# Fifteen loads of 1 to 15 rows of 64 bytes, put into the load queue between the first two K pieces and the first V piece

## The chip, the cores and the metric

The kernel runs on one core of a Trainium2 chip. The metric is the device time of one launch in microseconds (us). Engines are called as the profile calls them: PE (matrix multiply), DVE (vector), ACT (scalar activation), POOL, and SP, which here does nothing but issue loads. Loads move over the core's 16 DMA engines.

## What is computed

One decoding step, two batch rows (B = 2), everything in float32. Cut to what matters:

```python
xn = layernorm(x)                                   # x: 2 x 1 x 512
q = (xn @ wq)                                       # 32 heads of 128
p = softmax(einsum(q, k_cache) * 128**-0.5)         # k_cache: 2 x 32 x 8192 x 128
s = einsum(p, v_cache) @ wo                         # v_cache: the same shape
h = gelu(layernorm(xn) @ w1 + b1)                   # 512 -> 1376
g = silu(h @ w2 + b2)                               # 1376 -> 512
out = x + s * g
```

The two caches are 268 MB each, read once: nearly all of the 559 MB that the kernel reads.

## The kernel before

The caches are cut into N = 32 pieces each, of two heads: a piece is 128 partitions x 64 KB, 8.4 MB. K pieces go in turn to `big0` and `big1` (`KBUF`), V pieces to `big2` (`VB`). For every piece DVE multiplies K in place by q and reduces (`scores`, L319), PE and DVE find the maximum, ACT takes the exponentials, PE multiplies them with V (`weighted`, L466) and transposes the result. After the last V piece `wo` is loaded into `big2` in eight parts, and the projection ends the kernel.

Nearly all loads are issued by SP, in the order in which the program writes them, and a load that has to wait holds back all behind it:

- at the start the tail of `w2`, `w1`, `wq`, K piece 0 and the rest of `w2` (L202 to L212), one right behind the other;
- K piece 1 (L298), which waits for PE's last q product, because `wq` lies in its buffer;
- two loads of x into the tile `x4` (L299 to L301), each of 4 rows of 512 bytes;
- a wait (L304) for PE's last setup product (`pgate`), because the setup's operands lie in `big2`, and then V piece 0 (L305);
- from there in turn K piece n + 2, when PE is past the maximum of piece n (`p_k`), and V piece n + 1, when PE has read V piece n (`p_free`);
- at the end the last V piece in halves, `wo`, and the store of the output, with a wait for it (L373 to L375).

A load raises its semaphore by 16 when it is complete. `op` (L47) issues one instruction, `wait` (L39) only waits; both go through a helper, so the views show L51, L50 and L41 for nearly everything, and groups are told apart by their tiles.

Of the kernel before, what the change touches and what calls it, by code (L numbers as in the profile page):

```python
# [13 lines left out]
class Program:  # L14
# [24 lines left out]
    def wait(self, eng, *tokens):  # L39
        for name, v in self.need(eng, tokens):  # L40
            self.engines[eng].wait_ge(self.sem(name), v)  # L41
# [5 lines left out]
    def op(self, eng, method, *args, waits=(), sig=None, by=1, quiet=False, **kwargs):  # L47
        need = self.need(eng, waits)
        for name, v in need[:-1]:
            self.engines[eng].wait_ge(self.sem(name), v)  # L50
        ins = getattr(self.engines[eng], method)(*args, **kwargs)  # L51
        for name, v in need[-1:]:
            ins._wait_ge(self.sem(name), v)
        if quiet:
            return None
        name = sig or "own_" + eng
        by = 16 if method == "dma_start" else by
        ins.then_inc(self.sem(name), by)
        self.counts[name] += by
        return name, self.counts[name]  # L60


def decode_kernel(nc, x, kc, vc, wq, wo, w1, b1, w2, b2, out):
# [32 lines left out]
    op, wait, take = pr.op, pr.wait, pr.take  # L96

    def sb(shape, name):
        return nc.alloc_sbuf_tensor(name, list(shape), F32).ap()

    def ps(shape, name):
        return nc.alloc_psum_tensor(name, list(shape), F32).ap()
# [63 lines left out]
    rl = sb([P, B], "rl")  # L166
    on = sb([P, MB, OC], "on")
    mod_b = sb([P, R], "mod_b")

    bank = [ps([P, 512], f"bank{i}") for i in range(8)]  # L170
    po = bank[0]
# [18 lines left out]
    def pe(name):  # L190
        return "pe_setup", PE_EVENTS.index(name) + 1

    def pe_n(name, n):
        return name, n + 1

    t = {}
# [30 lines left out]
    for k in (7, 6, 1, 2, 4, 0):  # L227
# [13 lines left out]
                  op=ALU.add)  # L241
# [59 lines left out]
                     waits=[t["x4m"]])  # L301


    wait("SP", t["sel"], t["qnat"], pe(PE_EVENTS[-1]))  # L304
    op("SP", "dma_start", VB, vf[0], sig="d_v")  # L305
    for n in range(N - 2):
# [35 lines left out]
    with nc.scalar.Fori(0, N // U) as i:  # L342
        for u in range(U):
# [4 lines left out]
            for s in range(U):  # L348
# [19 lines left out]
                 op=ALU.mult, waits=[t["rl"], t["on0"], pe_n("p_oa", 0)])  # L368
# [3 lines left out]
    t["res"] = op("DVE", "tensor_add", res, res, x4, waits=[a, t["x4"]])  # L372
    t["out"] = op("SP", "dma_start", out.rearrange("b s (j n) -> j (b s) n", n=P), res[::HB, :], sig="d_out",  # L373
                  waits=[t["res"]])
    wait("SP", t["out"])  # L375


    done = []
# [23 lines left out]
    for c in range(ND):  # L402
# [4 lines left out]
        j, k = NF % QT, NF // QT  # L407
# [6 lines left out]
    j, k = NF % QT, NF // QT  # L414
    mm(ph[R * j:R * j + B, k * P:k * P + FT], ones[:1, :B], b1_sb[:, NF * P:], start=False, stop=True, sig="ph")
    by_tile = ident.rearrange("p (j r) -> p j r", r=R)
    for k in range(NH):
        n = min(QT, NF + 1 - k * QT)
# [16 lines left out]
    for g in range(N // NPB):  # L435
        mm(PB[g % len(PB)], sides, QN[:, g * NPB:(g + 1) * NPB, :].rearrange("h n d -> h (n d)"),
           waits=[t["side"], t["QN rest" if g else "QN first"]] + ([t[f"Q{QH}"]] if g >= len(PB) else []),
           sig=f"pb{g}")
    for f in range(NF + 1):
        j = f % QT  # L440
        k = P if f < NF else FT
# [3 lines left out]
    for j in range(QT):  # L445
        mm(pgate[R * j:R * j + MB, :], mod_b[:, :MB], g_nat[:, j * P:(j + 1) * P], waits=[t["g"], t["mod_b"]],
           sig="pgate" if j == QT - 1 else None)
# [64 lines left out]
    for b in range(B):  # L512
        h = slice(b * H, (b + 1) * H)
        mm(OA[:, b, :OC], Z[:, h].rearrange("p h r -> p (h r)"), mod, waits=[t["Z"]],
           sig="p_oa" if b == B - 1 else None)
# [45 lines left out]
```

## Time and profile before

| | us |
|---|---|
| median of 3 runs | 1300.24 |
| the three runs | 1300.05, 1300.24, 1301.04 |
| profiled execution, span from first to last instruction | 1298.7 |
| median less span (what lies around it) | 1.5 |
| PE busy | 461.9 (36%) |
| DVE busy | 1135.7 (87%) |
| ACT busy | 72.0 (6%) |
| DMA queue of SP and its packets, share of 16 engines | 99.7% |
| bytes read | 559.30 MB, 431 GB/s over the span |

The page's slices cut a span into 40 equal parts; a digit 9 says that the engine was busy for 90% of the slice or more. The same 40 slices are printed for any shorter window, so a window of 60 ns has slices of 1.5 ns and shows single packets. A packet is counted in the window in which it starts, with its whole duration and all its bytes; in a short window the share can so go over 100%, and GB/s far over what the engines move. The profiled execution's own time is not listed apart from the three runs.

### The profile page before, as it was taken

The numbers are of one execution on the slowest core, as the hardware profiler recorded it, in microseconds if no ns is written. First come the engines' busy times: TensorE is split into PE (matmuls) and PEld (weight loads), VectorE is DVE, ScalarE is ACT, GpSimd is POOL, SyncE is SP. The second block draws the span as 40 slices with busy tenths as digits, with TensorE's granted clock in tenths as the row PEclk, the third lists the DMA queues.
The fourth block names the chain that finished last, engine by engine and source line by source line (L and its number), as shares of the span: only waits on it lengthen the run. The fifth ranks groups of instructions, "written<-read, shape, count | busy, mean of one in ns | idle before, by whom it ended". The sixth has DMA issues, their size and how long they took to land. (4 is left out here: it accounts for less than half of the span.)

```text
span 1298.7 us, 7184 instructions
## 1 busy us (share of the span) xinstructions
PE 461.9 (36%) x2958; PEld 148.9 (11%) x2958; DVE 1135.7 (87%) x171; ACT 72.0 (6%) x245; POOL 2.1 (0%) x14
## 2 busy tenths in 40 slices
PE   3813434322433322343322344322334321333337
PEld 1201111001111000111000111100111100111103
DVE  2599999988889988889988888988888988888991
ACT  1100000000000000000000000000000000000000
POOL 0000000000000000000000000000000000000000
PEclk8756776667777567777556767656776666677659
DMA  9999999999999999999999999999999999999998
GB/s 412 436 426 444 424 440 430 426 446 424 444 426 430 440 426 446 424 442 426 426 446 426 444 426 438 430 426 446 426 444 424 438 432 426 446 424 442 416 432 360
DMA packets 11242, 559.38 MB, mean 431 GB/s; under 512 B 1264, under 2 KB 1536, under 8 KB 1892
## 3 DMA queue, kind: packets, MB, share of 16 engines
q1 hardware_dynamic: 11228, 559.30, 99.7%
q8 instruction: 3, 0.05, 0.0%
q14 instruction: 3, 0.02, 0.0%
q10 hardware_dynamic: 8, 0.01, 0.0%
HBM read 559.30 MB, written 0.00 MB: 431 GB/s over the span
## 5 line engine op out<-in xcount | busy, mean ns | idle before, releaser
L51 DVE TENSOR_TENSOR big<-big,Q 128x16384 f32<-128x16384 f32 (+1 forms) x33 | 551.3, 16707 | 73.5 <-DVEq L45 73.5
L51 DVE TENSOR_REDUCE sc<-big 128x128 f32<-128x16384 f32 (+1 forms) x33 | 551.2, 16703 | 4.8
L51 PE MATMUL bank<-big,PZ 128*8 128x512 f32 x2048 | 292.5, 735 | 629.2 <-PEq L45 629.2
L51 PEld LDWEIGHTS bank<-big,PZ 128*8 128x8 f32 x2048 | 60.5, 103 | 833.8 <-issue 833.8
L51 PE MATMUL bank<-Q,ident 128*128 128x512 f32 (+2 forms) x198 | 78.6, 507 | 0.2 <-issue 0.2
L51 ACT COPY o<-bank 128x512 f32<-128x512 f32 x33 | 19.3, 585 | 893.3 <-ACTq L45 881.7
L51 PE MATMUL bank<-ident,MX 128*1 128x128 f32 x32 | 9.2, 286 | 136.7 <-PEq L45 136.7
L51 PE MATMUL bank<-mod,o 128*128 128x2 f32 x256 | 32.8, 250 | 27.4 <-PEq L45 27.4
L51 PEld LDWEIGHTS bank<-mod,o 128*128 128x128 f32 x256 | 31.0, 191 | 55.4 <-issue 55.4
L51 PEld LDWEIGHTS bank<-Q,ident 128*128 128x128 f32 x198 | 33.6, 197 | 16.5 <-issue 16.5
L51 ACT ACTIVATE PZ<-sc,bias 64x128 f32<-64x128 f32 x64 | 25.5, 399 | 6.6 <-ACTq L45 6.2
L51 DVE TENSOR_REDUCE nm<-bank 1x2 f32<-1x128 f32 x32 | 8.9, 279 | 18.8 <-DVEq L45 18.8
L51 DVE TENSOR_TENSOR big<-big,mine 64x512 f32<-64x512 f32 (+1 forms) x2 | 4.5, 2279 | 21.8 <-ACT big L51 21.8
L51 PEld LDWEIGHTS bank<-ident,MX 128*1 128x1 f32 x32 | 2.5, 79 | 161.7 <-issue 161.7
L51 ACT COPY bias<-bank 128x1 f32<-128x1 f32 x32 | 5.1, 159 | 223.6 <-ACTq L45 223.6
L51 PE MATMUL bank<-big,sides 64*128 64x512 f32 x16 | 12.6, 962 | 3.7 <-DVE big L51 3.7
L51 PE MATMUL bank<-nm,srow 1*64 1x1 f32 x128 | 10.2, 216 | 9.8 <-PEq L45 9.4
L51 DVE TENSOR_REDUCE MX<-sc 128x1 f32<-128x128 f32 x32 | 9.2, 286 | 4.7
L51 PE MATMUL bank<-big,xnT 128*2 128x512 f32 x64 | 9.2, 744 | 10.6 <-DMA big<-in_A_wq_dram 10.6
L51 ACT ACTIVATION_READ_ACCUMULATOR PZ<-sc,bias x64 | 11.8, 185 | 0.0
L51 DVE SCALAR_TENSOR_TENSOR res<-bank,gate 128x128 f32<-128x128 f32 x1 | 0.3, 292 | 12.1 <-PE bank L51 12.1
L51 PEld LDWEIGHTS bank<-nm,srow 1*64 1x64 f32 x128 | 8.5, 160 | 16.1 <-issue 16.1
(78 smaller groups left out, 74.7 us busy)
## 6 DMA issues: line engine op xcount, KB each, us to landing
big<-in_A_k_cache_dram SPq DMA_DIRECT2D x2, 4096.0 KB, 35.9
big<-in_A_v_cache_dram SPq DMA_DIRECT2D x2, 4096.0 KB, 36.0
big<-in_B_w_dram SPq DMA_DIRECT2D x1, 2752.0 KB, 10.3
big<-in_B_w_dram SPq DMA_DIRECT2D x1, 2560.0 KB, 52.4
big<-in_A_wo_dram SPq DMA_DIRECT2D x1, 2560.0 KB, 14.9
big<-in_A_wo_dram SPq DMA_DIRECT2D x1, 2048.0 KB, 19.4
big<-in_A_wo_dram SPq DMA_DIRECT2D x1, 1536.0 KB, 22.6
big<-in_A_wo_dram SPq DMA_DIRECT2D x1, 1024.0 KB, 24.3
```

The source lines that it names most:

```text
L51: ins = getattr(self.engines[eng], method)(*args, **kwargs)
```

## The change

Between the two loads of `x4` and the wait before V piece 0, SP issues fifteen more loads. Load k (k from 1 to 15) brings 16 k values of x as k rows of 16 values, 64 bytes, into column block k of partitions 0 to k - 1 of a new tile `spare` (16 partitions x 1 KB). That makes 120 rows and 7,680 bytes. Nothing reads `spare`. The last wait of SP also asks that the fifteen loads are complete (15 x 16 = 240).

```diff
+    spare = sb([16, 16, 16], "spare")
...
+    for k in range(1, 16):
+        op("SP", "dma_start", spare[:k, k, :], x[0, 0, :16 * k].rearrange("(k n) -> k n", k=k), sig="d_spare")
     wait("SP", t["sel"], t["qnat"], pe(PE_EVENTS[-1]))
     op("SP", "dma_start", VB, vf[0], sig="d_v")
...
-    wait("SP", t["out"])
+    wait("SP", t["out"], ("d_spare", 240))
```

## Rows read from the trace of the kernel before

**Rows 1.** The page: busy us of the engines, DMA in 40 slices, SP's load queue.

```profile
PE 461.9 (36%) x2958; PEld 148.9 (11%) x2958; DVE 1135.7 (87%) x171; ACT 72.0 (6%) x245; POOL 2.1 (0%) x14
...
DMA  9999999999999999999999999999999999999998
...
q1 hardware_dynamic: 11228, 559.30, 99.7%
```

**Rows 2.** The DMA in 100 to 1200 us: totals, and issue to landing (median us).

```profile
DMA packets 8191, 476.98 MB, mean 434 GB/s; under 512 B 912, under 2 KB 912, under 8 KB 912
big<-in_A_v_cache_dram SPq DMA_DIRECT2D x29, 28.0
big<-in_A_k_cache_dram SPq DMA_DIRECT2D x28, 40.9
```

**Rows 3.** Timeline of SP, 0 to 110 us: start us, us, what it issued.

```profile
0.73 0.88 SPq L51 DMA_DIRECT2D big<-in_B_w_dram  x2
1.65 2.14 SPq L51 DMA_DIRECT2D big<-in_A_wq_dram  x1
...
40.70 0.33 SPq L51 DMA_DIRECT2D big<-in_A_k_cache_dram  x1
41.07 1.23 SPq L51 DMA_DIRECT2D x<-in_A_x_dram  x2
66.43 0.33 SPq L51 DMA_DIRECT2D big<-in_A_v_cache_dram  x1
```

**Rows 4.** The instructions that write or read tile x: duration ns min/median/max, starts.

```profile
L51 SPq DMA_DIRECT2D x<-in_A_x_dram x2: 509/588/668, 41.1 to 41.8; - x2
```

**Rows 5.** The DMA in 73.40 to 74.10 us (slices of 17.5 ns).

```profile
DMA  0000109109000990010199000091010990090000
DMA packets 40, 0.79 MB, mean 1129 GB/s; under 512 B 20, under 2 KB 28, under 8 KB 28
```

**Rows 6.** The DMA in 74.10 to 75.80 us (slices of 42.5 ns).

```profile
DMA  0000009000000000000000900009000000900000
DMA packets 8, 0.26 MB, mean 154 GB/s; under 512 B 4, under 2 KB 4, under 8 KB 4
```

**Rows 7.** The DMA in 73.45 to 73.51 us (slices of 1.5 ns).

```profile
DMA  3000900000000000000030009000000000030009
DMA packets 7, 0.00 MB, mean 26 GB/s; under 512 B 4, under 2 KB 7, under 8 KB 7
q1 hardware_dynamic: 7, 0.00, 12.2%
```

**Rows 8.** The DMA in 1293 to 1296 us (slices of 75 ns).

```profile
GB/s 328 342 423 341 341 314 410 178 273 219 219 109 164 150 82 137 96 109 82 82 109 96 82 68 41 55 27 14 27 27 0 0 0 0 0 0 0 0 0 0
```

**Rows 9.** The DMA in 1.75 to 2.00 us, the first packets of all.

```profile
DMA packets 20, 0.05 MB, mean 213 GB/s; under 512 B 1, under 2 KB 1, under 8 KB 19
q1 hardware_dynamic: 17, 0.03, 117.2%
```

**Rows 10.** Waits of SP: engine, line, releaser: us in total, times, longest.

```profile
SPq L51 <- PE bank L51: 1178.5, 62, 32.6
SPq L50 <- PE bank L51: 35.8, 1, 35.8
SPq L41 <- DMA out_dram<-res: 1.1, 1, 1.1
```

**Rows 11.** The DMA in 1272.5 to 1272.6 us: one packet of instruction code.

```profile
q14 instruction: 1, 0.01, 19.3%
```

**Rows 12.** Timeline of SP, 1200 to 1300 us.

```profile
1267.22 3.95 SPq L51 DMA_DIRECT2D big<-in_A_wo_dram  x8
```

**Rows 13.** The chain that ended last, in order of time: start us, us, what.

```profile
1269.32 25.18 DMA big<-in_A_wo_dram
...
1296.58 0.02 DVEq L50
```

## The prediction

> **What bounds the kernel now.** I read the page's slices first: the DMA row is 9 in every slice but the last, and SP's queue alone fills 99.7% of the 16 engines' time [rows 1]. DVE, the next, has 87% [rows 1]. So the 16 DMA engines set the time, and the question is whether they ever run dry. The DMA view of the steady part says no: at 434 GB/s one piece of 8.39 MB takes 8.39 / 0.434 = 19.3 us, while a V load lands 28.0 us and a K load 40.9 us after its issue [rows 2]. A V load so stands 28.0 - 19.3 = 8.7 us in the queue before its bytes move, a K load 21.6 us. SP does wait long for PE [rows 10], but those waits end before the queue is empty.
>
> Then I looked at how the 16 engines stand to each other where the change goes in, since each works off its own share of every load. At the border of K piece 1 and V piece 0 a completion mark (4 bytes) ends each engine's share of the one, and its first 64 KB packet of the other follows. Between 73.40 and 74.10 us there are 40 packets: 20 marks, 28 - 20 = 8 packets of 512 bytes, which are the 2 x 4 rows of the two `x4` loads, and 12 large ones [rows 5]. With 8 of the marks belonging to `x4`, 12 engines end K piece 1 here. In the next 1.7 us there are only 4 marks and 4 large packets, the last in slice 35, at 74.10 + 35 x 0.0425 = 75.6 us [rows 6]. So four engines trail by up to 75.6 - 73.45 = 2.1 us, and none of the trailing four carried a row of `x4`. At the end of the kernel the same spread is there: the rate falls from 1293.5 us on (slice 7) and is down to one engine's worth, 431 / 16 = 27 GB/s, from slice 26, and to nothing after slice 29, at 1295.25 us [rows 8]. The spread is 1.7 us, and for its last 0.3 us one engine works alone. That engine ends the kernel: the chain leads from its `wo` load [rows 13]. An engine that isn't the last has slack, and what is added to it is free up to that.
>
> **The change part by part.**
>
> *Fifteen issues on SP.* The two `x4` loads are the nearest rows: 0.51 and 0.67 us of SP each [rows 4], done at 41.07 + 1.23 = 42.3 us [rows 3]. Fifteen at the dearer price are 10.0 us and end at 52.3 us. What is queued behind them is the wait for PE and V piece 0, issued at 66.43 us [rows 3], the wait behind the 35.8 us row [rows 10]; so 14.1 us of cover are left. V piece 0 itself has further cover until the first engine is through with K piece 1, at 73.45 us [rows 7]: 7.0 us. The dearest issue in the trace, that of `wq`, took 2.14 us [rows 3]; fifteen of those are 32.1 us, end at 74.4 us and put V piece 0's first packet about 1.4 us later (0.33 us of issue, and from 0.73 to about 1.76 us between the first issue and the first packets [rows 3, 9]), 75.8 us, against 75.6 us for the trailing engine. I take 0, ends 0 and +0.2 us.
>
> *The rows on the DMA engines.* No 64-byte row is in the trace. The nearest is a 512-byte row of `x4`: in the window of 60 ns a mark stands in slice 0, a row in slice 4, a mark in slice 20, a row in slice 24 [rows 7]. One load with its mark so takes (24 - 4) x 1.5 = 30 ns of an engine. The seven packets hold 12.2% of 16 x 60 ns = 117 ns; 9 ns for each of 4 marks and 27 ns for each of 3 rows make 36 + 81 = 117. A 64-byte row lies between a 4-byte mark (9 ns) and a 512-byte row (27 ns): by proportion 9 + 18 x 60 / 508 = 11 ns, an estimate. The 30 ns step is 27 + 9 less 6 ns of overlap, so the step for 64 bytes is 11 + 9 - 6 = 14 ns, with ends 12 and 30 ns. The most loaded engine gets a row of all fifteen: 0.21 us (0.18 to 0.45).
>
> *Which engine pays.* The `x4` loads put their four rows on engines that are not the trailing ones. If load k takes its k engines from the same end, the four engines with most rows (12 to 15) have at least 75.6 - 74.1 = 1.5 us of slack, against at most 0.45 us. The last engine is then one of the other twelve and gets between 0 and 11 rows; I take the middle, 5.5 x 14 ns = 0.08 us. If the order were another, the last engine could get all fifteen: 0.45 us at most. Ends 0 and +0.45 us.
>
> The Trainium skill ("DMA: Bandwidth & Descriptors", section "Why a DMA increments its semaphore by 16 and not by 1") says that a load of k rows runs on as many engines as divide its row count, at most 16, and always the lowest-numbered ones. The 8 rows and 8 marks for two loads of 4 rows agree [rows 5]; by that rule the share of the last engine is the 0 to 11 rows above, and without it the 0.45 us end.
>
> *The new wait at the end.* It holds since about 75 us. A wait instruction alone on a queue shows as 0.02 us in the chain [rows 13]; I add 0.02 us (0 to 0.05) behind the 1.1 us wait for the store [rows 10].
>
> *What shifts in SP's program.* Fifteen more instructions may move a fetch of instruction code. One such packet held 19.3% of 16 x 0.1 us = 0.31 us of an engine [rows 11]; whether it meets the last engine is open either way. I take 0, ends -0.3 and +0.3 us. The `wo` issues keep their cover: issued by 1271.2 us [rows 12], moved until 1295.25.
>
> Sum: 0 + 0.08 + 0.02 + 0 = +0.1 us. The span of 1298.7 us becomes 1298.8. The median stands 1.5 us over the span for what lies around it, and nothing of the change touches that, so the median goes from 1300.24 to 1300.3 us.
>
> **The rivals.**
>
> *Slower, by small loads that don't overlap.* Place: the engine with fifteen rows, between its K piece 1 and V piece 0. In the forecast its packets follow one another at 14 ns, because the reads behind them are under way already. If each load waits for its own round trip, the price per load is far higher: the first 17 packets of the launch, 2 KB with nothing before them, took 1.172 x 16 x 0.25 / 17 = 0.28 us each [rows 9], and the store of the output, from the end of its issue to its completion, 1.1 us [rows 10]. Fifteen make 4.1 or 16.5 us on that engine, less its slack of some 1.6 us: 1302.8 or, at the full round trip, 1315.1 us. It decides (over 2.6 us, 0.2%) from (1.6 + 2.6) / 15 = 0.28 us per load. Against it: two `x4` loads followed each other with no such gap [rows 7], and both rows of one engine cost 60 ns. For it: two in a row are not fifteen.
>
> The same page of the Trainium skill (section "Latency and other measured facts") says that a tiny transfer can't go faster than a round trip to memory of about 800 ns. By that figure, if it held for each load in turn, the sum would be 15 x 0.8 - 1.6 = 10.4 us, or 1310.6 us, an estimate; rows 7 speak against that reading, since they show a step of 30 ns in a queue.
>
> *Slower, by a queue that takes only so many loads.* The trace shows at most some ten loads outstanding: the eight parts of `wo` and the last V halves [rows 12]. Here nineteen would be (`w2`, K piece 1, two of `x4`, fifteen). If SP stopped at ten, some eight small ones would be left until K piece 1 lands at 75.6 us: 8 x 0.6 us of issue and 1.4 us to V piece 0's first packet start all engines at 81.8 instead of 75.6 us: +6.2, 1306.4 us. Nothing in the trace shows such a stop.
>
> *The loads don't do what they say.* If they were dropped as unread or spread evenly, the time is that of before, 1300.2 us.
>
> *Faster.* The only thing to win is the trailing engine's lag, at most the 1.7 us of the tail [rows 8], or 1298.5 us, and a fetch of code elsewhere (0.3 us). Rows added behind K piece 1 take nothing from the engine that trails already.
>
> **How the numbers follow.** Forecast 0.90; loads that don't overlap 0.05; a full queue 0.02; dropped loads 0.01; faster 0.02. The likeliest gives 1300.3 us. Its bounds: below, 1300.24 - 0.3 for the fetch and some 0.4 for what medians of such runs do (the three span 1.0 us), so 1299.5; above, 0.2 + 0.45 + 0.05 + 0.3 for the costs and the same 0.4, so 1301.6. That holds over 8 in 10 without the rivals. About 0.2%, 2.6 us, is what a measurement of this kernel can tell from no change; the forecast and the dropped loads lie within it, 0.91; both queue rivals are slower, 0.07; faster 0.02.
>
> **What would show it.** After should have 120 rows and 120 marks more, 11,482 packets; SP busy with the new loads from 42.3 to 50 or 52 us and V piece 0 still issued at about 66.4 us; between 73.4 and 75.8 us trains of small packets at 14 ns on engines that come early, up to 0.2 us long, and the last first packet of V piece 0 still at 75.6 to 75.7 us. Wrong would be: gaps of tenths of a microsecond between the small packets, V piece 0 issued after 73.4 us, a longer spread at the end than 1.7 us, or a change of the rate between 100 and 1200 us.

## The result, and the profile after

| | before | after |
|---|---|---|
| median of 18 runs, us | 1300.07 | 1301.37 |
| ratio after / before, 95% interval | | 1.0013 [1.0007, 1.0019] |
| span of the profiled execution, us | 1298.7 | 1300.0 |

One run of 1361.88 us among the 18 after is left out of the ratio. The change costs 1.3 us. That is inside the range on record (1299.5 to 1301.6) and under 0.2%, but the interval leaves out 1, so it is a loss that can be measured, where the forecast was no difference to speak of (+0.1 us).

The steady part didn't change. The DMA view of 100 to 1200 us answers [rows 2]: 434 GB/s as before, a V load lands as long after its issue as before.

```profile
DMA packets 8190, 476.86 MB, mean 434 GB/s; under 512 B 912, under 2 KB 912, under 8 KB 912
...
big<-in_A_v_cache_dram SPq DMA_DIRECT2D x29, 28.1
```

SP is not it either. Its timeline (start us, us, what) answers [rows 3]: the fifteen issues take 5.37 us, and V piece 0 is issued at 67.3 us, 6 us before its bytes can move.

```profile
41.48 5.37 SPq L51 DMA_DIRECT2D spare<-in_A_x_dram  x15
67.26 0.36 SPq L51 DMA_DIRECT2D big<-in_A_v_cache_dram  x1
```

The border between K piece 1 and V piece 0 is where the time went. These are the DMA views of 73.60 to 74.90 us and of 74.90 to 76.00 us, which answer [rows 5] and [rows 6].

```profile
DMA packets 256, 0.86 MB, mean 664 GB/s; under 512 B 235, under 2 KB 243, under 8 KB 243
...
q1 hardware_dynamic: 256, 0.86, 221.7%
...
DMA packets 32, 0.20 MB, mean 180 GB/s; under 512 B 29, under 2 KB 29, under 8 KB 29
...
q1 hardware_dynamic: 32, 0.20, 50.3%
```

There are 264 packets under 512 bytes: 120 rows, 120 marks of the new loads, 24 marks of K piece 1 and `x4`; and the first 64 KB packets of V piece 0, 13 + 3 = 16. The shares make 2.217 x 16 x 1.3 + 0.503 x 16 x 1.1 = 55.0 us of packet time. The small packets hold 2.8 us of it (11 ns a row, 9 ns a mark, 27 ns for each of 8 rows of `x4`), so a first packet took 52.2 / 16 = 3.26 us on average. A 64 KB packet in the steady part takes 2.42 us. The trains themselves are as short as forecast; the packet behind a train is what is late.

Two of the trailing engines show whom that hits. The DMA views of 75.20 to 75.45 us (slices of 6.25 ns), of 75.31 to 75.34 us and of 75.40 to 75.45 us:

```profile
DMA  1010102222291010101090000000000000000109
...
DMA packets 4, 0.07 MB, mean 2187 GB/s; under 512 B 3, under 2 KB 3, under 8 KB 3
...
q1 hardware_dynamic: 4, 0.07, 780.2%
...
q1 hardware_dynamic: 4, 0.07, 306.4%
```

A row with its mark comes every two slices, 13 ns (14 were forecast). The train that is under way at 75.20 us ends with its 64 KB packet in slice 20, at 75.33 us; it began at 75.20, so it has ten rows. That packet, with three small ones (29 ns) in the second view, took 7.802 x 16 x 0.03 - 0.029 = 3.72 us. The last engine of all starts its packet in slice 39, at 75.44 us, behind a single row between two marks, and takes 3.064 x 16 x 0.05 - 0.029 = 2.42 us, as ever. So the former ends its packet at 75.33 + 3.72 = 79.05 us, the latter at 77.86 us: the last engine but one has become the last, by 1.2 us. In the kernel before, the last engine's first packet ended at 75.6 + 2.42 = 78.0 us [rows 6], 1.0 us earlier.

A packet of instruction code adds to this. One (queue q14) is moved at 151.11 us and lasts 0.31 us (19.3% of 16 x 0.1 us in the view of 151.05 to 151.15 us). The 64 KB packet that starts on its heels, in the view of 151.41 to 151.42 us, takes 17.506 x 16 x 0.01 = 2.80 us and ends at 154.21 us, where the last mark of that border stands (view of 154.1 to 154.3 us, slices of 5 ns, slice 22):

```profile
q1 hardware_dynamic: 1, 0.07, 1750.6%
...
DMA  0000000000000000000000190000000000000000
```

In the kernel before, the view of 152.9 to 153.1 us has the last mark of this border at 152.98 us. So in these two executions the last engine is 1.2 us later at this border, where it was 1.0 us later at the first: about 0.2 us of the loss goes by way of the code packet.

The tail, here the GB/s of 1293 to 1297 us in slices of 100 ns, keeps that to the end: [rows 8] ended at 1295.25 us, this ends in slice 35, at 1296.55 us, 1.3 us later.

```profile
GB/s 584 246 338 502 348 338 441 317 318 348 246 338 236 256 215 225 164 225 205 154 154 143 154 102 133 92 154 123 72 92 82 72 62 41 51 31 0 0 0 0
```

### The profile page after: what moved, and what is told of

It is laid out like the page before. It is cut to its first block, busy times and chain, and to the rows that moved or that the text cites. A ratio compares the mean times of both kernels' runs of the same rounds, so it can differ in the third digit from the quotient of the medians.

```text
span 1300.0 us, 7199 instructions
## 1 busy us (share of the span) xinstructions
PE 464.1 (36%) x2958; PEld 150.1 (12%) x2958; DVE 1135.7 (87%) x171; ACT 72.0 (6%) x245; POOL 2.1 (0%) x14
## 5 line engine op out<-in xcount | busy, mean ns | idle before, releaser
L51 ACT COPY o<-bank 128x512 f32<-128x512 f32 x33 | 19.3, 586 | 898.7 <-ACTq L45 887.1
```

## The experiments

Theory A, formed on these rows: each small load on an engine costs the packet behind the train about 0.2 us, after some five that are covered; the kernel pays what its last engine pays.

**Loads 1 to 5 alone, and loads 6 to 15 alone.** The count in SP's last wait is matched in each.

```diff
-    for k in range(1, 16):
+    for k in range(1, 6):        # the other run: range(6, 16)
```

> Only loads 1 to 5 of the fifteen (15 rows in all; at most five rows on one engine). Theory A, the stall: an engine's first 64 KB packet behind a train of small loads is late by about 0.2 us for each small load over the first five or so; the trailing engines have none of these rows, or one. A: time as before, within 0.3 us, and no first packet of V piece 0 over 2.6 us. Rival B, the loads cost by their mere presence (a shifted program, a code fetch, a wait at the end): +0.5 to +1.3 us here too. Rival C, chance of the launch (the spread of the engines differs from launch to launch): no fixed order between this and the others.

> Only loads 6 to 15 (105 rows; ten on each of the first six engines, then nine falling to one). Theory A: the second of the trailing engines has ten rows, as with all fifteen, and its first 64 KB packet of V piece 0 takes some 3.7 us in place of 2.42; the time is that of the full change, +1.0 to +1.4 us over before. Rival B: about the same as for loads 1 to 5. Rival C: as there.

Measured: loads 1 to 5 give 1299.81 us against 1300.04 (0.9999 [0.999, 1.0008]), loads 6 to 15 give 1301.17 us (1.001 [1.0001, 1.0019]). The whole loss is in the later ten loads, those that put ten rows on the first six engines. That speaks against a price for the loads' presence, for the longer program or for the added wait (rival B). It speaks against the chance of the launch (rival C) as well: the eleven runs of the one, 1299.52 to 1300.23 us, and the eleven of the other, 1300.49 to 1301.79 us, don't overlap.

Theory A was off in two things. With loads 1 to 5 it expected no first packet over 2.6 us. One took 18.60 x 16 x 0.01 - 0.009 = 2.97 us, in the view of 74.07 to 74.08 us; that engine carries the two loads of `x4` too, and so seven small loads, and it had the slack.

```profile
q1 hardware_dynamic: 2, 0.07, 1860.0%
```

With loads 6 to 15, no first packet of a trailing engine took 3.7 us. On one of them the time stands between the small rows instead, in the view of 75.80 to 77.03 us (slices of 31 ns; a 2 or 4 is a small row with its mark, a large number a 64 KB packet of another engine):

```profile
GB/s 0 0 0 0 0 2 0 0 0 0 0 0 0 0 0 0 0 0 0 0 2131 2 0 0 2131 0 0 0 2131 0 2 0 0 0 0 0 2 0 0 4
```

Small packets stand in slices 5, 21, 30, 36 and 39: steps of 0.49, 0.28, 0.18 and 0.09 us in place of 13 ns. The same loss can so show in either form, and the records don't decide which packet it belongs to.

**The fifteen loads one by one.** One load ahead of each of V pieces 1 to 15, in place of all ahead of V piece 0.

```diff
...
         load_k(n + 2, pe_n("p_k", n))
+        k = n + 1
+        if k < 16:
+            op("SP", "dma_start", spare[:k, k, :], x[0, 0, :16 * k].rearrange("(k n) -> k n", k=k), sig="d_spare")
```

> All fifteen loads, but one ahead of each of the V pieces 1 to 15 in place of all ahead of V piece 0. Theory A: no train is longer than one small load, so no first packet is late; only the 13 ns steps stay, up to 0.2 us: time as before, -0.2 to +0.3 us. Rival B (presence): +1.3 us as with all at once. Rival D, every small load costs 0.1 to 0.2 us of an engine wherever it stands: +0.8 to +2.2 us.

Measured: 1300.07 us against 1300.04 (1.0002 [0.9993, 1.0011]). The same 120 rows cost nothing that can be measured when no train is longer than one load. Rival D, a price of 0.1 to 0.2 us for every small load wherever it stands, expected 0.8 us or more. The interval alone leaves out only the upper part of that, but the spans settle it: all eleven lie between 1298.5 and 1299.0 us, 0.2 us over the kernel before at the median (1298.7 against 1298.5), which is what fifteen steps of 13 ns make.

**Fifteen rows on every engine, and on the first four only.** Fifteen loads of 16 rows each, or of 4 rows each.

```diff
-    for k in range(1, 16):
-        op("SP", "dma_start", spare[:k, k, :], x[0, 0, :16 * k].rearrange("(k n) -> k n", k=k), sig="d_spare")
+    for k in range(15):
+        op("SP", "dma_start", spare[:, k, :], x[0, 0, :256].rearrange("(k n) -> k n", k=16), sig="d_spare")
```

> Fifteen loads of 16 rows each at the place of the change, so every engine gets fifteen rows, the last one too. Theory A: every engine's first packet of V piece 0 is late by about 2.1 us, plus 0.2 us for the train; nothing covers it on the last engine: +2.0 to +2.6 us over before. Rival E, the stall comes from many engines reading the same KB of x at once: worse than in proportion, first packets over 5 us, +3 us or more. Rival B: +1.3 us.

> Fifteen loads of 4 rows at the place of the change: fifteen rows on each of the four engines that also carry the rows of x4, and which trail nobody; none on the others. These four lose some 2.0 us (15 loads x 0.2 us, less the five that are covered) plus the train's 0.2 us, and have 1.5 to 2.1 us of slack. If only the last engine counts: +0.1 to +0.7 us over before, well under the +2.5 us of fifteen rows on every engine. If a late engine's loss is the kernel's loss whoever it is: +2.2 us.

Measured: 16 rows give 1302.6 us against 1300.04 (1.0022 [1.0013, 1.0031]), +2.6 us, at the upper end of what A expected. 4 rows give 1301.66 us against 1299.92 (1.0015 [1.0006, 1.0024]), +1.7 us. That is less than on all engines, but far over the 0.1 to 0.7 us expected: this expectation was wrong. The DMA views of 131.4 to 134.4 us (slices of 75 ns) and of 150.7 to 154.7 us (slices of 100 ns) show where the time goes, at the border of K piece 3 to V piece 2 and at the next one.

```profile
DMA  0999099990900000000009990000000009999909
...
DMA  0999199990000000999000000999099990090000
...
q14 instruction: 1, 0.01, 0.5%
```

At the first border the three engines that used to come last start V piece 2 in slices 21 to 23. The four with the fifteen rows start it in slices 33 to 39, where the second packets of the leading engines stand too. So the four have lost all of their slack and are the last now, by 16 slices, 1.2 us. They carry the two loads of `x4` ahead of the fifteen, so seventeen small loads, which the expectation left out. At the second border the engines that used to be last stand in slices 16 to 18 and the last one in slice 35: 17 slices, 1.7 us, as much as the kernel lost. In between one 8 KB packet of instruction code was moved, 0.5% of 16 x 4 us = 0.3 us. The last engine lost about 0.5 us there, so the code packet fell on one of the engines that had just become the last. In the run of the full change, too, a code packet made an engine the last.

**How the price grows.** Trains of 2 to 15 loads, ahead of V pieces 3, 6, 9, 12, 15, 18 and 21 of one kernel, without the fifteen loads of the change: as separate loads of 16 rows of x; as one load of so many rows per engine; as separate loads from addresses 32 KB apart; as separate loads with rows of 512 bytes.

```diff
         load_k(n + 2, pe_n("p_k", n))
+        if n % 3 == 2 and n // 3 < 7:
+            m = (2, 4, 6, 8, 10, 12, 15)[n // 3]
...
+            for i in range(m):   # one load: spare[:, :m, :16] <- wo[:16 * m, :16]
+                op("SP", "dma_start", spare[:, i, :], x[0, 0, :256].rearrange("(k n) -> k n", k=16), sig=f"d_spare{m}")
```

> Trains of 2, 4, 6, 8, 10, 12 and 15 loads of 16 rows of 64 bytes of x, so that each engine gets one row per load, ahead of V pieces 3, 6, 9, 12, 15, 18 and 21. Theory A (about 0.2 us for each small load over some five that are covered): the first 64 KB packets behind the trains are late by 0, 0.05, 0.2, 0.9, 1.3, 1.7 and 2.2 us on every engine; in all about 6 us slower than before. If instead a train of any length has one price, all seven stalls are alike.

> The same trains of 2 to 15 rows of 64 bytes per engine, but each train is one load (16 partitions x 2 to 15 rows, out of wo), so that only one completion mark stands behind it. If the price is that of the rows (small reads): stalls as with separate loads, 6 us slower in all. If it is that of the marks, or of a load as such: no first packet late by more than 0.1 us, and the time as before to 0.5 us.

> The same trains of 2 to 15 loads of 16 rows of 64 bytes, read 32 KB apart out of wo in place of one KB of x. If engines hold each other up at the same addresses, the stalls go to near nothing; by theory A (price per load, wherever it reads) they stay at 0 to 2.2 us, 6 us in all.

> The same trains of 2 to 15 loads of 16 rows, with rows of 512 bytes in place of 64, out of wo. If the price belongs to rows under 512 bytes, no first packet is late by more than 0.1 us, and only the rows' own 27 + 9 ns each are paid (57 rows x 30 ns = 1.7 us in all). By theory A, a price per load whatever its size, the stalls are those of 64 bytes less what the longer rows cover, 12 x 16 ns each at most: 1.1 us at ten loads, 1.9 us at fifteen.

Measured, one run of each against one of the kernel before (1299.57 us): 1305.97, 1301.27, 1305.98 and 1308.18 us. In the views of the borders all sixteen first packets stand in one window; here those with separate loads of x at 8, 10 and 15 (538.3 to 540.25, 655.0 to 656.9 and 889.75 to 892.0 us), then one load of 15 rows per engine (887.4 to 889.7 us), then 15 loads from distant addresses (889.75 to 892.0 us).

```profile
q1 hardware_dynamic: 288, 1.06, 164.5%
...
q1 hardware_dynamic: 352, 1.06, 201.8%
...
q1 hardware_dynamic: 512, 1.06, 211.7%
```

```profile
q1 hardware_dynamic: 288, 1.06, 124.4%
```

```profile
q1 hardware_dynamic: 512, 1.06, 210.2%
```

Worked out as above (share x 16 x window, less 11 ns a row and 9 ns a mark, over 16 packets), a first packet takes 3.04, 3.63 and 4.45 us behind 8, 10 and 15 loads: late by 0.62, 1.21 and 2.03 us. From 8 to 15 loads that is 1.41 / 7 = 0.20 us per load, and the line meets zero at 15 - 2.03 / 0.2 = 4.9 loads. Six and twelve loads, worked out the same way from the views of 421.7 to 424.0 and of 772.2 to 774.1 us, make 0.33 and 1.50 us, near the same line. Behind one load of 15 rows a first packet takes 2.68 us, late by 0.26; behind 15 loads from distant addresses 4.42 us, late by 2.00. So the price goes with the loads, hardly with the rows, and not with the address. The trains of one load each still cost 1.7 us in all, more than the 0.5 us expected: 57 rows of 11 ns are 0.6 us of it, the late first packets are a part, and a single run doesn't place the rest. The price doesn't vanish with longer rows either: rows of 512 bytes cost 8.6 us in all against 6.4, more by the 57 x 16 ns = 0.9 us that the longer rows themselves take and some 1.3 us that these runs don't place.

**Longer trains, and wider loads.** Trains of 15, 20, 25 and 30 loads of 16 rows; and trains of 2 to 10 loads of 128 rows of 128 bytes.

```diff
-            m = (2, 4, 6, 8, 10, 12, 15)[n // 3]
+            m = (15, 20, 25, 30)[n // 3]      # wider: (2, 4, 6, 8, 10), wo[128 * i:128 * i + 128, :32]
```

> Trains of 15, 20, 25 and 30 loads of 16 rows of 64 bytes of x ahead of V pieces 3, 6, 9 and 12. A price per load of 0.2 us beyond a cover of five: late by 2.0, 3.0, 4.0 and 5.0 us, 14 us in all. If the loss is one round trip to memory that a long train only uncovers (at most some 2.2 us): all four late by 2.0 to 2.5 us, 9 us in all.

> Trains of 2, 4, 6, 8 and 10 loads of 128 rows of 128 bytes out of wo: eight rows per engine and load, so that one load keeps an engine busy for some 80 ns in place of 13. If a load holds its engine for 0.2 us whatever it moves, its own rows count towards that: at eight loads train and stall together stay at 0.7 us, at ten at 1.3 us. If the price comes on top of the rows: 1.3 us at eight, 2.0 us at ten.

Measured: the long trains 1314.71 us against 1299.92, +14.8 us, where a price per load expected 14 and a single uncovered round trip 9. So the price goes on. By the first packets it is somewhat smaller in these trains: behind 20 loads, in the view of 307.7 to 309.9 us with 320 rows and 336 marks, a first packet takes 5.06 us, late by 2.64; behind 30, in the view of 545.6 to 549.8 us, 6.59 us, late by 4.17 (939 small packets of 10 ns, and two of the 18 large ones are ordinary packets of 2.42 us).

```profile
q1 hardware_dynamic: 672, 1.07, 248.6%
...
q1 hardware_dynamic: 957, 1.21, 178.1%
```

From 20 to 30 loads that is 0.15 us per load, and less than the 3.0 and 5.0 us expected. That the total came out so near is therefore in part luck; these runs don't place the difference.

The wide loads gave 1303.78 us, +3.9 us for 30 loads. With up to 8 x 13 + 9 = 113 ns of own packets per load, a load that holds its engine for the longer of its own time and the price would make some 3.5 us, a price on top of the own time over 5. The run is nearer to the former but decides neither; this stays open.

**The same loads from another queue.** Fifteen loads of 16 rows, issued by ACT behind its last setup instruction.

```diff
...
     t["th"] = op("ACT", "activation", th, z, AF.Tanh, scale=0.5, waits=[t["z"]])
+    for k in range(15):
+        op("ACT", "dma_start", spare[:, k, :], x[0, 0, :256].rearrange("(k n) -> k n", k=16), sig="d_spare")
```

> The fifteen loads of 16 rows, issued by ACT behind its last setup instruction (from about 67 us) in place of SP, so that they go through ACT's own load queue on the same 16 engines, while K piece 1 moves. If a small load holds the engine itself for 0.2 us: +2.0 to +2.6 us over before, as from SP. If it only holds up what stands behind it in its own queue, SP's large packets fill the time: only the rows' and marks' own 15 x 13 ns stay, 0 to +0.5 us.

Measured: 1300.38 us against 1300.1 (1.0001 [0.9992, 1.001]), where the same loads from SP cost 2.6 us. The DMA view of 73 to 134 us has both queues (packets, MB and share), that of 60 to 140 us the small loads (issue to landing, median us):

```profile
q1 hardware_dynamic: 480, 26.22, 99.8%
q10 hardware_dynamic: 464, 0.02, 0.5%
...
spare<-in_A_x_dram ACTq DMA_DIRECT2D x15, 1.0 KB, 33.3
```

The small loads take 33 us each to land now, and nothing waits for them; SP's queue keeps the engines full meanwhile. So the 0.2 us is not time in which an engine can do nothing else: SP's large packets stood in another queue, and they lost nothing. One thing stays open. SP's 26.22 MB are some 400 packets of 64 KB, and 464 small packets of ACT's queue went by in the same time, about one to one. The small loads no longer passed the engines as a train, as little as in the run with one load ahead of each V piece. Whether a train in one queue would hold up another queue isn't shown.

## Why the prediction was wrong

**What bounds the kernel: right.** The DMA engines do, and the last of them ends the kernel; an engine that leads has slack. Loads 1 to 5 alone show it, and the two tails show it at the end. The rate of the steady part stayed, as forecast. That the measured time lies inside the range is luck: the allowances for SP, a code packet and the runs' scatter cover for the rows' term, whose own upper end was 0.45 us.

**Fifteen issues on SP: right.** 5.4 us, cheaper than the 10 us allowed, and all of it covered.

**The rows on the DMA engines: the step that failed.** The step of a row with its mark was put at 14 ns and is 13. But that was taken for the whole price, on the strength of two `x4` loads that followed each other without a gap [rows 7]. Two loads lie inside the cover of about five, where any price is hidden; the row could not show the price per load, 0.2 us, and it was not asked what the 64 KB packet behind the train does. The mis-sized term is 0.08 us for the last engine, with an upper end of 0.45; with ten loads it is 0.13 + 0.2 x (10 - 4.9) = 1.2 us, and 1.4 us was measured on the engine that had them (3.72 - 2.42 us, and 0.13 of train).

**Which engine pays: half right.** The last engine at this border was one of the twelve with fewer rows, as forecast. But the middle of the twelve was taken for it. The former last had one row, and the last but one ten: with a staircase the question is not what a typical trailing engine gets, but which of them comes last with its own share added. Nor was the slack of the engines with most rows enough. One of the leading engines starts its first packet at 74.196 us, in the view of 74.19 to 74.20 us with two small packets, and takes 28.75 x 16 x 0.01 - 0.020 = 4.58 us, late by 2.2. It ends at 78.78 us, 0.9 us behind the engine that used to be last and 0.3 us ahead of the one with ten rows.

```profile
q1 hardware_dynamic: 3, 0.07, 2875.0%
```

**The wait at the end: right, nothing seen of it** in the runs with five or with spread loads. **The program's shift:** the prediction named the code packets, left them at 0 and allowed 0.3 us either way. They cost when they meet an engine that is the last or near it, some 0.2 us here and 0.5 us with the four-row loads.

**The rivals.** "Small loads that don't overlap" was the right mechanism at the right place and got 0.05. Its price was taken from the first packets of the launch (0.28 us) and the output's round trip (1.1 us) [rows 9, 10], both too dear, and its cover, one engine's slack, was counted for the engine with fifteen rows alone. At 0.2 us it gives +1.2 us by the engine with ten, which is below the 2.6 us from which the prediction counted a loss, so even as a rival it would have been put down as no difference. The reading of the Trainium skill ("DMA: Bandwidth & Descriptors", section "Latency and other measured facts"), that 800 ns for each load in turn would make 10.4 us, is not borne out: the runs show 0.2 us per load beyond five. The rule on which engines a load takes (same page, section "Why a DMA increments its semaphore by 16 and not by 1") fits the runs: loads 1 to 5 left the trailing engines alone, and fifteen loads of 4 rows made four engines the last. No view here numbers the engines. The full queue fell: thirty loads were outstanding in the long trains with nothing but the price per load.

## What to carry to other kernels

Ahead of a large load, count the small loads in its queue, not their bytes: here a train beyond about five cost the next packet about 0.2 us per load and engine (0.15 between 20 and 30 loads). Spread them between large loads, make one load of many rows of them, or issue them from a queue in which nothing urgent stands behind: each of the three cost little or nothing here. And where all engines are busy to the end, ask first which engine is the last and what the edit puts on that one and on those close behind it.

## What was not expected of the hardware

- Rows of 64 bytes pass an engine at 13 ns with their mark, but each load beyond the fifth or so delays what stands behind it in the queue by 0.15 to 0.2 us; the records show this as a longer 64 KB packet (6.59 us on average behind 30 loads, in place of 2.42) or as gaps between the small ones.
- From ACT's queue fifteen loads on all engines cost nothing measurable, against 2.6 us from SP's; there they passed about one to each 64 KB packet of SP's. Whether the delay lies in the load itself or in its completion mark isn't shown, since every load here has one mark, and why it begins only beyond about five loads isn't either.
- A packet of instruction code (8 KB, 0.3 us) costs an engine more than its own time: the 64 KB packet right behind it took 2.80 us in place of 2.42.
- The spread between engines that the launch leaves stays to the end: 2.1 us at 75 us [rows 5, 6], 1.7 us at 1295 us [rows 8].
